# Packed attention and a soft mixture on one core: loads admitted earlier, a new order of the work, and a tail whose first four tiles need no reduction

## The chip, the cores and the metric

One core of one Trainium2 chip. The number is the device time of one execution in microseconds (us), lower is better. Before the change three runs gave 197.42, 199.47 and 200.94 us; the median is 199.47 us.

## The reference

Eight batches, eight heads, 576 tokens, head size 64, all float32. Per head 32 learned rows `p` attend to keys and values, and the 576 queries then attend to those 32 packed rows. The result, laid out as 4608 tokens by 512, goes through a soft mixture of 8 experts with 4 slots each.

```python
p_packed = sm_attn(p, k, v)                    # 32 rows per head
x = sm_attn(q, p_packed, p_packed)             # 4608 x 512 after the transpose of heads
logits = x @ phi                               # 4608 x 32 slots
slot_input = softmax(logits, over tokens).T @ x
slot_out[e] = relu(slot_input[e] @ w1[e]) @ w2[e]      # 512 -> 1024 -> 512, 4 rows per expert
out = softmax(logits, over slots) @ slot_out
```

The weights are 16 MB in `w1` and 16 MB in `w2`; with q, k and v and the output the core moves 72.31 MB.

## The kernel before, in words

The program has two parts. The **attention part** works in eight steps: step i takes two batches and four heads (`k{i}`, `q{i}`, `v{i}`, each in two transfers of 576 KB). Its pieces are functions `f_...`, and the table `ORDER` names them one by one; each piece puts its instructions at the end of its engines' queues, so the table is the order of every engine. A token `s1.3.0@4:a` is piece `s1`, step 3, part 0, PSUM bank 4, copy on ScalarE (`v`: VectorE, `p`: GpSimd). The pieces of a step:

- `kt` turns keys on VectorE; `s1` scores of `p` against keys; `mx1`, `e1` maximum and exponential; `ap`/`apc` turn the weights by TensorE and copy them out; `m` product with values; `ppa`, `pp`, `pt`, `ptc` scale, turn and store the packed rows; `mp`/`mm` their product with `phi`.
- `qp`/`qc` turn queries by TensorE and copy them out; `s2` scores of queries against the packed rows; `mx2`, `sb`, `e2`, `z2`, `rc`, `n2` their softmax (`z2`, `n2` on GpSimd or VectorE); `a2p`/`a2c` turn the result; `lg` adds a step's share of the logits.
- After every second step (a pair) come `f1`, `f2`, `f3`, `f5`, `f6`, `fd`, `fl`, `gz`, `gr`, `rt`, `gt`, `rb`, `gs`, `sa`: the running softmax over tokens and the pair's share of `slot_input`. After the last pair this chain ends in `xz` (line 1076), the input of the first expert layer.
- `w.4.0@7` multiplies ones by ones into a free bank and nothing reads it.

The **expert part** is plain code: `layer1a` and `layer1b` (W1), `layer2` (W2 of experts 0 to 5, 512 columns wide), then `last2` for the last two experts by column halves x = 0 and 1. W2's partial sums stand on four groups of 32 partitions. `total(x)` (VectorE) adds the halves' sums into `so`, `spread(x)` (TensorE, a product with the table `rep`) adds the four groups, and `shared(x)` (ScalarE) copies the result to `sh`. An output tile of 128 tokens is one product of its 32 combine weights `cT` with `sh` (`part`), a copy (`keepp`) and a share of a transfer (`send`). Of the 36 tiles the first 16 are made in column halves, the other 20 whole. `f_cp`/`f_cc` turn the combine weights into `cT`; the third group (`f_cp(2, ...)`) stands after `spread(1)`.

**Loads** are issued by SyncE in one list. The list may run ahead only as far as `ALLOW` says: the products and turns are counted (4 and 2 units), the count passes a mark at 194 and then every 256 units (`FIRST`, `BLOCK`), and entry n of `ALLOW` is the number of transfers that may be issued before mark n + 1 has passed. A transfer also waits for its place: a ring of 120 KB per partition, or, for the weights, places 0 to 5 and x in the work area (`PLACE`), given free by `late.*` and `lx` in `ORDER`; and it waits for the eighth transfer before it. W2 of experts 6 and 7 is loaded by column halves, in rows of 1 KB.

Of the kernel before, what the change touches and what calls it, by code (L numbers as in the profile page):

```python
# [31 lines left out]
ptc.1.1:v ptc.1.0:a z2.0.0:p mp.1.0 mx1.2.0 w.1.0@5 mm.1.0:a s2.1.0@5 kt.3.0 e1.2.0 s2.1.1 kt.3.1
e1.2.1 rc.0.0 ra.2.0 qp.2.1@0 mx2.1.2 qp.2.3@1 n2.0.0:p qc.2.1:a qp.2.2@2 qc.2.3:a ap.2.1@0 qc.2.2:a
kt.3.2 qp.2.0@4 apc.2.1:a qp.2.4@3 sb.1.2 qp.2.5@2 qc.2.0:a a2p.0.0@0 qc.2.4:a qc.2.5:a a2p.0.2@1
a2p.0.1@3 a2c.0.0:a rz.2.0 kt.3.3 ap.2.2@2 e2.1.0 ap.2.0@0 apc.2.2:v s1.3.0@4 a2c.0.1:a z2.1.0:p
s1.3.1 apc.2.0:a a2c.0.2:a m.2.0@2 mx1.3.0 m.2.1 m.2.2 e1.3.0 rc.1.0 e1.3.1 lg.0.0@1 n2.1.0:v
ppa.2.1 ap.3.1@0 ra.3.0 ap.3.0@7 ppa.2.0 apc.3.1:a ap.3.2@6 pp.2.1 apc.3.0:a a2p.1.2@5 kt.4.1
# [1216 lines left out]
```

## Time and profile before

| | |
|---|---|
| time of the profiled execution | 198.95 us |
| its span, first to last instruction | 196.8 us |
| median of three runs | 199.47 us |
| TensorE busy | 167.2 us (85%) |
| VectorE busy | 124.1 us (63%) |
| ScalarE busy | 89.7 us (46%) |
| GpSimd busy | 35.7 us (18%) |
| moved by DMA | 72.31 MB, mean 367 GB/s |

The busy shares are means over stages that have different limits: the attention part ends and the first expert layer starts at about 136 us, the weights are loaded until about 170 us, and from 184 us on only output is moved. So the rows are read by stage, and for each stage the question is which wait ends last.

### The profile page before, as it was taken

The page shows a single profiled execution, that of the slowest core. Times are in us where ns is not written, and L with a number is a line of the kernel's source. Part 1 is how long each engine was busy: PE and PEld are TensorE (multiplying, and loading weights), DVE is VectorE, ACT ScalarE, POOL GpSimd, SP SyncE. Part 2 cuts the span into 40 slices and gives each one's busy share as a digit, 9 for nine tenths or more (in the row PEclk, how much of TensorE's full clock was granted, in tenths as well). Part 3 has the DMA queues.
Part 4 walks back from the last instruction along what each step waited for, and adds up shares of the span by engine and source line. Part 5 has one row for each costly group of instructions (what it writes and reads, how often), then busy time and mean ns, then how long its engine had stood idle before and what let it go on. Part 6 is the DMA issues. An engine that isn't in the chain of part 4 may idle for free.

```text
span 196.8 us, 6563 instructions
## 1 busy us (share of the span) xinstructions
PE 167.2 (85%) x2841; PEld 108.9 (55%) x2841; DVE 124.1 (63%) x261; ACT 89.7 (46%) x229; POOL 35.7 (18%) x61
## 2 busy tenths in 40 slices
PE   7978986999999999999999989687999997979100
...
GB/s 182 377 388 284 388 395 371 214 358 383 390 367 387 394 392 375 354 351 411 410 407 406 342 407 414 417 421 397 382 425 420 399 350 348 205 341 341 441 420 244
DMA packets 29228, 72.31 MB, mean 367 GB/s; under 512 B 2192, under 2 KB 10896, under 8 KB 27408
## 3 DMA queue, kind: packets, MB, share of 16 engines
q1 hardware_dynamic: 29200, 71.90, 97.3%
...
## 4 chain that ended last, share of the span: by engine, by line
PE 34%; DVE 25%; DMA 17%; ACT 9%; issue 3%; SPq 3%; POOL 1%; DVEq 0%; ACTq 0%; POOLq 0%
PE ps L150 31%; DMA ring<-in_k_dram 10%; DMA ring<-in_moe_w_dram 4%; DVE work L448 4%; ACT work L397 4%; PE ps L153 4%; DMA ring<-in_q_dram 3%; DVE work L401 3%; DVE mx L656 3%; SPq L159 3%; DVE ring L401 2%; ACT work L480 2%; DVE nm L477 1%; DVE work L666 1%; DVE zs L716 1%
## 5 line engine op out<-in xcount | busy, mean ns | idle before, releaser
L397 ACT COPY work<-ps 128x512 f32<-128x512 f32 (+3 forms) x68 | 30.0, 487 | 21.7 <-PE ps L153 18.3
L150 PE MATMUL ps<-work 128*64 128x64 f32 (+1 forms) x1088 | 34.0, 313 | 1.7 <-ACT work L397 0.7
L150 PEld LDWEIGHTS ps<-work 128*64 128x64 f32 (+1 forms) x1088 | 24.1, 122 | 10.0 <-issue 2.5
L448 DVE STREAM_TRANSPOSE work<-ring 128x576 f32<-128x576 f32 x32 | 23.3, 755 | 5.9 <-DMA ring<-in_k_dram 5.7
L153 PE MATMUL ps<-ident,ring 128*128 128x128 f32 x144 | 20.6, 280 | 0.1
L150 PE MATMUL ps<-ring,work 64*64 64x128 f32 x576 | 18.3, 273 | 2.2 <-issue 2.0
L150 PEld LDWEIGHTS ps<-ring,work 64*64 64x64 f32 x576 | 15.7, 133 | 4.8 <-issue 3.8
L397 ACT COPY a2Tb<-ps 128x384 f32<-128x384 f32 x21 | 9.8, 497 | 16.5 <-PE ps L153 16.3
L153 PEld LDWEIGHTS ps<-ident,ring 128*128 128x128 f32 x144 | 15.9, 141 | 2.5 <-DVE work L401 0.7
L480 ACT ACTIVATE work<-ps,nm 128x576 f32<-128x576 f32 x16 | 11.8, 739 | 11.9 <-DVE nm L477 11.8
L153 PE MATMUL ps<-ident,work 128*128 128x128 f32 x108 | 15.3, 279 | 1.9 <-ACT work L480 1.5
L656 DVE TENSOR_REDUCE mx<-ps 128x36 f32<-128x1152 f32 (+1 forms) x10 | 11.0, 1100 | 7.5 <-PE ps L150 7.5
L150 PE MATMUL ps<-a,a2Tb 32*128 32x256 f32 (+2 forms) x112 | 13.6, 505 | 2.0 <-DVE a2Tb L401 1.3
L401 DVE COPY ring<-ps 128x256 f32<-128x256 f32 (+1 forms) x25 | 11.3, 514 | 5.7 <-PE ps L150 5.6
L153 PEld LDWEIGHTS ps<-ident,work 128*128 128x128 f32 x108 | 11.8, 141 | 4.9 <-ACT work L480 3.4
L150 PE MATMUL ps<-ring,hT 128*32 128x512 f32 (+1 forms) x136 | 13.2, 496 | 0.3
L397 ACT COPY ring<-ps 128x256 f32<-128x256 f32 (+1 forms) x27 | 10.6, 483 | 5.9 <-PE ps L150 5.9
L150 PE MATMUL ps<-ones 128*128 128x512 f32 (+2 forms) x24 | 12.1, 615 | 1.0 <-DVE ones L118 1.0
L401 DVE COPY work<-ps 128x384 f32<-128x384 f32 (+3 forms) x24 | 11.5, 484 | 2.2 <-PE ps L153 1.8
L150 PE MATMUL ps<-ring,a2Tb 128*32 128x512 f32 x96 | 12.4, 594 | 0.4 <-DVE a2Tb L1076 0.4
L477 DVE TENSOR_REDUCE nm<-ps 128x2 f32<-128x1152 f32 x8 | 10.8, 1349 | 2.6 <-PE ps L150 2.6
L703 POOL TENSOR_TENSOR zt<-work 128x576 f32<-128x576 f32 x3 | 4.3, 1417 | 38.4 <-ACT work L695 38.4
...
## 6 DMA issues: line engine op xcount, KB each, us to landing
ring<-in_moe_w_dram SPq DMA_DIRECT2D x22, 1024.0 KB, 9.3
...
work<-in_moe_w_dram SPq DMA_DIRECT2D x6, 1024.0 KB, 12.2
...
```

Of the source, the lines that this page charges most:

```text
L150: return step(nc.tensor.matmul(*a, **k), 4)
L153: return step(nc.tensor.transpose(*a, **k), 2)
L159: x = nc.sync.dma_start(out=dst, in_=src).ins
L397: nc.scalar.copy(dst, src)
L401: nc.vector.tensor_copy(dst, src)
L448: nc.vector.transpose(kT[:, b2, :, c].rearrange("p m (t r) -> p m t r", t=T), view(f"k{i}.{b2}").rearrange("p (m t c d) -> p m t c d", m=2 ...
L477: nc.vector.tensor_reduce(nms[i % 2], s1v(i), axis=AX.XY, op=ALU.max, negate=True)
L480: nc.scalar.activation(a1[:, :, x].rearrange("p t (h r) -> p h t r", h=2), s1v(i)[:, x].rearrange("p h (t r) -> p h t r", t=T), AF.Exp, bi ...
L656: nc.vector.tensor_reduce(mxs[i % 2][:, a0:a1].rearrange("p a t -> p (a t)"), s2v(i, j).rearrange("p a t s -> p (a t) s"), axis=AX.X, op=A ...
L666: nc.vector.tensor_tensor(a2s[i // NG % 2][:, :, i % NG, a0:a1].rearrange("p t a s -> p a t s"), s2v(i, j), mxs[i % 2][:, a0:a1].unsqueeze ...
L703: nc.gpsimd.tensor_tensor(y, a[:, :, :, 0:w], a[:, :, :, w:NS], op=ALU.add)
L716: nc.vector.reciprocal(z, z)
```

## The change

Four edits. `ALLOW` is raised by 1 or 2 in twelve of its sixteen entries. `ORDER` is written anew (as many pieces; 13 products of ones where 12 stood), and `PLACE` gives places 0 and 1 to other weight chunks. W2 of expert 6 is loaded in one whole first half (rows of 8 KB) and two column halves of the rest. In the tail, `repf` times `cT` gives `wide`, the combine weights of tiles 0 to 3 repeated over 128 partitions; `direct` multiplies them with `so`, so that these tiles need neither `spread` nor `shared`. Twelve tiles are halved instead of 16, in other sends, and all three `f_cp` stand between the `layer2` calls.

```diff
-ALLOW = (24, 24, 24, 27, 31, 34, 39, 43, 47, 51, 55, 57, 60, 62, 64, 66)
+ALLOW = (24, 24, 24, 28, 33, 36, 41, 44, 49, 52, 57, 58, 61, 62, 65, 67)
-PLACE = "rrrrrrrrr01rrr2rr345x"
+PLACE = "rrrrrr01rrrrrr2rr345x"
 ORDER = """
-p.0.0 w.4.0@7 w.1.0@7 px.0.0@0 pc.0.0:a kt.0.0 kt.0.1 kt.0.2 kt.0.3 w.4.0@7 w.4.0@7 w.1.0@7 s1.0.0@0
+p.0.0 w.4.0@7 w.1.0@7 px.0.0@0 pc.0.0:v kt.0.1 kt.0.0 kt.0.3 kt.0.2 w.4.0@7 w.4.0@7 w.1.0@7 qp.0.0@0
...
     cuts = {
-        (E - 2, 0): (0, 4, 8),
+        (E - 2, 0): (4, 8),
         (E - 1, 0): (0, 4, 6, 8),
-        (E - 2, 1): (0, 8),
+        (E - 2, 1): (4, 8),
...
+    f_cp(0, 0, 6, None)
+    f_cc(0, 0, None, "v")
     layer2(3)
+    f_cp(1, 0, 7, None)
+    f_cc(1, 0, None, "a")
     layer2(4)
+    f_cp(2, 0, 4, None)
+    f_cc(2, 0, None, "v")
+    wide = a2f[:, 3 * DM : 4 * DM]
+    for a in range(4):
+        rs = slice(32 * a, 32 * a + 32)
+        product(ps[:, a, 0:P], repf[rs], cT[rs, 0], start=True, stop=True)
+    copy("a", wide.rearrange("p (a x) -> p a x", a=4), ps[:, 0:4, 0:P])
     layer2(5)
+    layer2(E - 2)
...
+    def direct(t, x, b):
+        product(
+            ps[:, b, 0:HB], wide[:, P * t : P * (t + 1)], so[:, halves[x]], start=True, stop=True
+        )
...
+    ends_a = (1, 2, 4, 6, 9, 12)
+    ends_b = (1, 2, 4, 6, 9, 12)
...
+    def lead(x):
+        total(x)
+        direct(0, x, (pa, pb)[x][0])
+        direct(1, x, (pa, pb)[x][1])
+        spread(x)
+        direct(2, x, (pa, pb)[x][2])
+        direct(3, x, (pa, pb)[x][3])
+        keep_tile(0, x, "a")
+        keep_tile(1, x, "v")
+        shared(x)
+        keep_tile(2, x, "v")
+        keep_tile(3, x, "a")
...
     last2(E - 2, 0)
     last2(E - 1, 0)
-    total(0)
-    spread(0)
-    shared(0)
     obs[1] = rows(1)
-    ends_a = (1, 2, 4, 9, 12, 16)
-    ends_b = (2, 4, 9, 16)
+    lead(0)
     tiles(4, 8, 0)
     last2(E - 2, 1)
     tiles(8, 12, 0)
     last2(E - 1, 1)
-    total(1)
-    tiles(12, 16, 0)
-    spread(1)
-    f_cp(2, 0, 4, None)
-    shared(1)
-    tiles(0, 4, 1)
-    f_cc(2, 0, None, "v")
+    lead(1)
```

TensorE at the start of the program, after the first products of ones (`ps<-ones`). `ident,ring` are turns of queries, `work 32x288` are the scores `s1`. Before:

```order
L150 MATMUL ps<-ones 128x512 x2
L150 MATMUL ps<-ones 128x128
L150 MATMUL ps<-work 32x288 x32
L153 MATMUL ps<-ident,ring 128x128 x18
L150 MATMUL ps<-ones 128x512
L153 MATMUL ps<-ident,work 128x128 x9
```

and now:

```order
L150 MATMUL ps<-ones 128x512 x2
L150 MATMUL ps<-ones 128x128
L153 MATMUL ps<-ident,ring 128x128 x9
L150 MATMUL ps<-work 32x288 x16
L153 MATMUL ps<-ident,ring 128x128 x5
L150 MATMUL ps<-work 32x288 x16
L153 MATMUL ps<-ident,ring 128x128 x4
L150 MATMUL ps<-ones 128x512 x2
L153 MATMUL ps<-ident,work 128x128 x9
```

Nine query turns of step 0 moved ahead of its first scores, and two products of ones follow the last query turns where one stood.

VectorE around the softmax of the last step's queries (`mx_172`, `zs_174`), ahead of the last `lg`. `nml`, `nm_176` and `low_137` are `f1` and `f3` of the third pair; `d`, `L_sb` are its `fd`, `fl`. Before:

```order
L764 TENSOR_REDUCE nml<-ps 128x1
L768 SCALAR_TENSOR_TENSOR nm_176<-nml,low_138,own 128x4
L656 TENSOR_REDUCE mx_172<-ps 128x18
L788 TENSOR_REDUCE low_137<-ps 128x1
L666 TENSOR_TENSOR a_1_109<-ps,mx_172 128x2x9x32
L656 TENSOR_REDUCE mx_172<-ps 128x18
L807 STREAM_TRANSPOSE d<-rt 128x288
L666 TENSOR_TENSOR a_1_109<-ps,mx_172 128x2x9x32
L812 STREAM_TRANSPOSE L_sb<-ps 128x288
L700 TENSOR_REDUCE zs_174<-a_1_109 128x9x2 x2
```

and now:

```order
L654 TENSOR_REDUCE mx_172<-ps 128x18
L664 TENSOR_TENSOR a_1_109<-ps,mx_172 128x2x9x32
L654 TENSOR_REDUCE mx_172<-ps 128x18
L664 TENSOR_TENSOR a_1_109<-ps,mx_172 128x2x9x32
L698 TENSOR_REDUCE zs_174<-a_1_109 128x9x2
L713 TENSOR_SCALAR zs_174<-zs_174 128x9x2
L714 RECIPROCAL zs_174<-zs_174 128x9x2
L698 TENSOR_REDUCE zs_174<-a_1_109 128x9x2
L713 TENSOR_SCALAR zs_174<-zs_174 128x9x2
L714 RECIPROCAL zs_174<-zs_174 128x9x2
L718 TENSOR_TENSOR a_1_109<-a_1_109,zs_174 128x9x64
L762 TENSOR_REDUCE nml<-ps 128x1
```

The third pair's chain, which stood between the pieces of this softmax, now follows it.

TensorE behind the last `lg` (`a2Tb,mm_157`), up to the last pair's `gr` (`a_1_109,d`). `work,d` is the third pair's `gr`, `rep,rt` its `gt`, `rb,pp` its `gs`. Before:

```order
L150 MATMUL ps<-a2Tb,mm_157 32x288 x4
L150 MATMUL ps<-ones 128x384
L150 MATMUL ps<-nm_176,rep 128x4
L150 MATMUL ps<-ones 128x512
L150 MATMUL ps<-rw,ones 128x64
L150 MATMUL ps<-a_1_109,d 32x256 x16
```

and now:

```order
L150 MATMUL ps<-a2Tb,mm_157 32x288 x4
L150 MATMUL ps<-rw,ones 128x64
L150 MATMUL ps<-work,d 32x256 x18
L150 MATMUL ps<-nm_176,rep 128x4
L150 MATMUL ps<-rep,rt 64x32 x8
L150 MATMUL ps<-ones 128x256
L150 MATMUL ps<-rb,pp_152 64x64 x2
L150 MATMUL ps<-rb,pp_153 64x64 x2
L150 MATMUL ps<-rw,ones 128x64
L150 MATMUL ps<-a_1_109,d 32x256 x16
```

The third pair's `gr`, `gt` and `gs` stand here now, and two products of ones are gone.

## Rows read from the trace of the kernel before

**Rows 1.** The page, parts 3 and 5: a DMA queue; a group of VectorE copies.
```profile
q1 hardware_dynamic: 29200, 71.90, 97.3%
...
L401 DVE COPY work<-ps 128x384 f32<-128x384 f32 (+3 forms) x24 | 11.5, 484 | 2.2 <-PE ps L153 1.8
```

**Rows 2.** Windows: length, busy us of each engine, TensorE clock, DMA share, GB/s.
```profile
core 0: us, PE busy (x) PEld busy (x) DVE busy (x) ACT busy (x) POOL busy (x), PEclk, DMA share, GB/s
36.00:112.00 76.00, 73.94 (x1607) 58.60 (x1608) 61.04 (x115) 47.08 (x123) 20.41 (x19) 1.00 1.01 376
112.00:136.00 24.00, 19.18 (x297) 12.77 (x299) 17.92 (x48) 11.69 (x33) 7.17 (x9) 1.00 1.02 413
34.00:37.00 3.00, 2.71 (x86) 1.38 (x64) 1.85 (x3) 1.52 (x3) 1.90 (x2) 1.00 0.56 154
80.00:86.00 6.00, 5.85 (x113) 4.17 (x111) 5.14 (x13) 3.83 (x11) 0.00 (x0) 1.00 0.96 321
139.00:155.00 16.00, 16.00 (x164) 5.45 (x160) 8.63 (x23) 2.50 (x5) 0.00 (x0) 1.00 1.01 421
156.00:167.00 11.00, 9.68 (x92) 3.32 (x88) 1.31 (x3) 1.22 (x3) 0.00 (x0) 1.00 1.08 349
168.00:172.00 4.00, 4.00 (x53) 1.84 (x53) 2.26 (x6) 1.46 (x5) 0.00 (x0) 1.00 0.53 178
```

**Rows 3.** The chain that ended last: start us, us, engine, tile, line.
```profile
19.13 8.66 DMA ring<-in_k_dram
...
27.88 0.78 DVE work L448
...
47.87 1.36 DVE work L720
...
116.84 0.32 DVE nml L764
117.19 0.93 DVE nm L768
...
120.58 0.39 DVE d L807
...
121.60 0.39 DVE L_sb L812
...
123.99 0.41 DVE a2Tb L401
...
135.91 16.61 PE ps L150 x160
...
165.09 0.44 DVE a L1133
165.57 0.71 PE ps L150 x2
166.36 0.38 ACT a L397
```

**Rows 4.** Timeline of TensorE: start us, us, line, operation, tiles, count (two instructions per product).
```profile
121.66 1.49 PE L150 MATMUL ps<-work,d 64*32 64x256 f32 x36 [0.26 <-DVE a L666]
...
127.59 0.69 PE L150 MATMUL ps<-a2Tb,mm 128*32 128x288 f32 x8 [0.30 <-ACT a2Tb L397]
...
159.17 1.90 PE L150 MATMUL ps<-ring,hT 128*32 128x512 f32 x16
...
161.81 3.24 PE L150 MATMUL ps<-ring,hT 128*32 128x256 f32 x32
...
168.67 1.07 PE L150 MATMUL ps<-ring,hT 128*32 128x256 f32 x16
...
172.49 0.53 PE L153 MATMUL ps<-ident,L_sb 128*128 128x128 f32 x3
```

**Rows 5.** Waits of SyncE's queue: us in total, times, longest.
```profile
SPq L159 <- PE ps L150: 80.8, 22, 9.4
```

**Rows 6.** DMA issues between 136.9 and 137.2 us: KB, us to landing.
```profile
ring<-in_moe_w_dram SPq DMA_DIRECT2D x1, 1024.0 KB, 5.1
```

More of the change, by code (lines that the diff above doesn't have):

```diff
@@ L32 @@
[L32 to L37, printed above, removed]
@@ new lines @@
+qp.5.4@2 ppa.6.1 ap.7.0@7 qc.5.4:a pp.6.1 ra.7.0 s2.5.0@4 apc.7.0:v ppa.6.0 pp.6.0 rz.7.0 a2p.4.2@7
+pt.6.0 a2c.4.2:a a2p.4.1@2 ptc.6.0:v ptc.6.1:a s2.5.1 a2c.4.1:a mp.6.0 mx2.5.2 qp.6.1@7 mm.6.0:a
+qp.6.3@3 qc.6.1:a qp.6.5@0 qc.6.3:a sb.5.2 qp.6.4@7 qp.6.2@1 qc.6.5:a qp.6.0@2 qc.6.2:a ap.7.1@0
+qc.6.4:v e2.5.0 qc.6.0:v a2p.4.0@6 ap.7.2@7 apc.7.1:v s2.6.1@4 a2c.4.0:a apc.7.2:v z2.5.0:p s2.6.0@6
+mx2.6.1 sb.6.1 qp.7.4@0 qp.7.3@1 qc.7.4:v e2.6.7 mx2.6.0 qp.7.5@5 qp.7.1@0 rc.5.0 lg.2.0@4 qc.7.1:a
@@ new lines @@
+sb.6.0 z2.6.7:p m.7.0@2 qc.7.5:v e2.6.6 m.7.1 late.2.0 qc.7.3:v m.7.2 z2.6.6:p rc.6.7 qp.7.0@1
+ppa.7.1 ppa.7.0 pp.7.1 qp.7.2@0 pp.7.0 qc.7.0:v pt.7.0 qc.7.2:a n2.6.7:p ptc.7.1:v ptc.7.0:a rc.6.6
+s2.7.1@0 n2.6.6:p s2.7.0@5 late.3.0 mx2.7.1 n2.5.0:p sb.7.1 a2p.6.1@7 mx2.7.0 e2.7.7 a2p.6.2@1
+a2p.6.0@0 a2c.6.2:a sb.7.0 mp.7.0 a2c.6.0:a a2p.5.2@1 z2.7.7:v mm.7.0:a e2.7.6 a2p.5.0@0 a2p.5.1@3
+a2c.5.2:a rc.7.7 a2c.5.0:a z2.7.6:v n2.7.7:p a2c.5.1:a a2c.6.1:a rc.7.6 lg.2.1 n2.7.6:v lg.3.0@7
+f1.2.0 a2p.7.1@3 xz.0.0 a2p.7.0@0 a2c.7.1:a f2.2.0 a2c.7.0:a a2p.7.2@6 f3.2.0 f5.2.0 a2c.7.2:v
@@ L1063, in layer2 @@
     def layer2(e):
-        for j in range(NJ):
+        for j in range(NJ if e < E - 2 else NJ // 2):
             a = j % 4
@@ L1124, in last2 @@
                 w2h(e, j, x),
-                start=(e == E - 2 and j < 4),
+                start=(e == E - 2),
                 stop=(e == E - 1 and j >= 4),
@@ L1167, in send, with keep_tile, tiles @@
         nc.sync.dma_start(out=ov[:, t0:t1, xs], in_=ob[:, t0:t1, xs])
+    def direct(t, x, b):
+        product(
+            ps[:, b, 0:HB], wide[:, P * t : P * (t + 1)], so[:, halves[x]], start=True, stop=True
+        )
+    pa = (4, 6, 7, 5, 0, 4, 6, 7, 5, 0, 2, 4)
+    pb = (6, 7, 5, 0, 2, 4, 1, 6, 7, 5, 0, 2)
+    NA = len(pa)
+    ends_a = (1, 2, 4, 6, 9, 12)
+    ends_b = (1, 2, 4, 6, 9, 12)
+    def keep_tile(t, x, eng):
+        keepp(t, x, (pa, pb)[x][t], eng)
+        ends = (ends_a, ends_b)[x]
+        if t + 1 in ends:
+            send(max(n for n in (0, *ends) if n <= t), t + 1, x)
+    def tiles(t0, t1, x):
+        for t in range(t0, t1):
+            part(t, x, (pa, pb)[x][t])
+        for t in range(t0, t1):
+            keep_tile(t, x, "av"[t % 2])
+    def lead(x):
[10 more added lines that the diff above has]
+        keep_tile(3, x, "a")
     nc.vector.tensor_copy(sot[:, halves[0]], ps[:, SO, halves[0]])
@@ L1196, in pack_attention_soft_moe @@
     last2(E - 1, 1)
-    total(1)
-    tiles(12, 16, 0)
-    spread(1)
-    f_cp(2, 0, 4, None)
-    shared(1)
-    tiles(0, 4, 1)
-    f_cc(2, 0, None, "v")
-    for t in range(4, NA, 4):
-        tiles(t, t + 4, 1)
-    obank = (0, 2, 4, 6, 7, 5, 1, 3)
+    lead(1)
+    tiles(4, 8, 1)
+    tiles(8, 12, 1)
+    obank = (3, 4, 1, 6, 7, 5, 0, 2)
     work = {"a": 0.0, "v": 0.0}
```

100 lines of the change are left out of this document (39 added, 61 removed).

## The prediction, made before the changed kernel ran

> **What bounds the kernel now.** I read the DMA queues first, then the windows by stage, then the chain of waits, then the timeline of TensorE around the two ends of the expert part. The queue of the loads is occupied 97.3% of the span [rows 1], so the first guess is that bytes set the time. The windows say how far that is true: the DMA moves 421 GB/s with rows of 8 KB, 349 with rows of 1 KB, and falls to 154, 321 and 178 in short stretches [rows 2]. Against 376, the mean of 36 to 112 us, these hold idle time of 3 x (1 - 154/376) = 1.8 and 6 x (1 - 321/376) = 0.9 us, and, against 349, 4 x (1 - 178/349) = 2.0 us. SyncE spends most of its waiting on TensorE's products, 80.8 us in 22 waits [rows 5]: `ALLOW` and the places hold loads back, no lack of data.
>
> The chain decides what such a wait costs. Until 27.8 us it consists of transfers that wait for no product; from 27.88 to 152.5 us no transfer stands in it, only TensorE, VectorE, ScalarE and GpSimd [rows 3]. So computation sets the start of layer 1, which I call S (135.91), and the weights that need a place freed by layer 1 start only after it. Within that stretch TensorE is busy 73.94 of the 76 us from 36 to 112 and 19.18 of the 24 us from 112 to 136 [rows 2]. Behind S both bind: TensorE's last products ahead of `total(0)` take 3.24 us for 32 instructions where 16 of the same shape take 1.07 [rows 4], so 1.1 us of them is waiting for the last weights, and the end is the DMA sending output.
>
> The sums stand against the profiled execution, 198.95 us (its span is 196.8); the median of three runs is 0.52 higher, and the forecast is the median less the gain.
>
> **Loads further ahead.** Before S they fill up to 1.8 + 0.9 = 2.7 us of idle DMA. I count 0 for it: no step between 27.9 us and S waits for a transfer, so this work hides it entirely; were computation to become faster by more than that, the cover would be gone and loads would be late next. Behind S it shortens the queue that the last weights stand in: a transfer of 1 MB issued just after S lands 5.1 us later [rows 6], while its bytes at 421 GB/s take 2.5. The gain there lies between 0 and 2.6 us; I take 1.4, about the middle, since a transfer into an empty queue needs some time too before its bytes flow.
>
> **The order up to S.** At the start nine query turns precede the first scores, so these begin later, by the wait for q and the turns. Nothing for it, as the chain waits for the keys of step 2 until 27.8 us in any case; without that cover it would cost the turns and the wait, some 2 us. From 36 to 112 us the same products and turns run in another order on an engine that idles 2.06 us there; I take 0, between a gain of 2.06 and a loss by VectorE. That loss is bounded by the copies: VectorE gets 13 more of them (13 x 0.484 = 6.3 us by its mean copy [rows 1]) and gives up two `n2` (2 x 1.36 [rows 3]), a `z2` of that size and one half as large (2.0), net 1.6 us.
>
> From 112 us to S something moves that stands in the chain. Between the scores of the last queries and the last `lg` (127.59 [rows 4]) VectorE now works off, in the chain, `f1` of the third pair (0.32 + 0.93), its `fd` and `fl` (0.39 + 0.39) and a copy for `lg` (0.41), together 2.44 us [rows 3]. The copy goes to ScalarE; the rest moves behind the softmax. `f1` comes back ahead of the last `lg`, as 0.6 us: -1.8. The last scores also start earlier, since nine turns (`a2p` of step 5) and one `lg` move behind them; one `lg` is 0.69 us [rows 4], and the way through `m`, `pp`, `pt`, `ptc` doesn't shrink, so I take -0.9. Behind the last `lg`, S follows after 135.91 - 127.59 = 8.3 us. The third pair's `gr` now stands on TensorE in there, ahead of the last pair's `f2`: 1.49 us [rows 4], of which the 0.6 of `f1` would be waited for anyway, so +0.9; with two products of ones gone I take +0.8. `gt` and `gs` stand where TensorE waits for the last pair's `f3` and `f5`, and I count them at 0; without that cover they cost their own length. Sum: S - 1.9, between -4.0 (with the 2.06) and +1.6.
>
> **From S to `total(0)`.** It starts at S + 29.18 now (165.09); without its 1.1 us of waiting TensorE would be there at S + 28.1. Added on TensorE: the third group of `cT` turns (0.53), the four products for `wide` (at most the 0.53 of four products of 256 columns) and four products of 512 columns instead of 256 (0.95 - 0.53) [rows 4]: S + 29.6. By the loads it would be 29.18 - 1.4 + 1.0 (1 MB of whole rows, 2.5 us at 421, lands ahead where 0.5 MB of half rows, 1.5 us at 349, did) = 28.8, at worst 30.2. TensorE is the later one: +0.4.
>
> **From `total(0)` to the end.** Two things. One MB of output leaves in whole rows: 3.0 us at 349 against 2.5 at 421, -0.5. The Trainium skill says in "DMA: Bandwidth & Descriptors", Specifications, that transfers reach line rate from 512 B on, so rows of 1 KB should lose nothing and this term would be 0. The trace shows 349 against 421 here and disagrees; by the rule the forecast would be 0.5 us higher. Second, idle DMA at 168 to 172 us, 2.0 us: outputs are not ready. The first tiles now skip `spread` and `shared` (166.74 - 165.57 = 1.2 us in the chain [rows 3]), tiles 4 and 5 leave without tile 8, and the third `cp` with its copy no longer stands in front of the second half's tiles. Some idle time stays between the small sends: I take -1.0, between 0 and -2.0. Together -1.5.
>
> **Sum:** -1.9 + 0.4 - 1.5 = -3.0: 195.9 in the frame of the profiled execution, 199.5 - 3.0 = **196.5 us** against the median.
>
> **Rivals.**
> 1. Nothing gained before S. For it: TensorE at 97% over 76 us can't be beaten by order, and the third pair's chain comes back between the last `lg` and S, in full if it doesn't overlap. Against it: 2.44 us of VectorE in the chain have left. Time: 0.4 - 1.5 = -1.1: 198.4. That the loads don't run ahead in effect, because the place or the eighth transfer before stops them, ends here too.
> 2. The whole order is better. The 2.06 us of idle TensorE between 36 and 112 us go as well, S - 4.0, which the 2.7 us of filled DMA and the queue behind S allow in part. For it: VectorE is busy only 61 of those 76 us, so its waits are latency, and latency is what an order changes. Against it: little idle time is left to take. Time: -4.0 + 0.4 - 1.5 = -5.1: 194.4.
> 3. Slower: VectorE becomes the bound in the attention part. In-order copies ahead of `mx2`, `kt` and `nm` delay `s1` and `s2`, the added 6.3 us fall on the path and the removed 4.7 us lie off it. It decides as soon as TensorE's idle time in the 76 us grows past the 1.1 us that the tail gives back. Price up to 6.3 - 1.1 = +5.2, 204.7; halfway, +3.2 - 1.1, 201.6. For it: in the whole stretch from 36 us to S VectorE has 79 of 100 us already. Against it: ScalarE's share goes down by as many copies.
>
> **Chances and range.** Forecast 0.45, rival 1 0.22, rival 2 0.21, rival 3 0.12. A measurement of this kernel tells about 2% from no change, which is 195.5 and 203.5 us. Faster: nearly all of rival 2 and 0.3 of the forecast, whose own spread (the idle time after `total(0)`, the queue at S) is about 1.2 us either way: 0.34. Slower: the upper half of rival 3, 0.06. Within: 0.60. The range for 8 in 10 takes in rivals 1 and 2 with their spread and leaves out most of rival 3 and the far end of rival 2: 193.2 to 200.0.
>
> **What would show it.** S near 134 us, with the last `lg` about 9 us ahead of it and no `f1`, `fd`, `fl` in the chain between the last scores and the last `lg`; DMA windows without the drops to 154 and 321 GB/s; TensorE without a gap before `total(0)`, which comes 29.6 us after S; 31.7 - 1.5 = 30.2 us from `total(0)` to the end of the span. It is wrong if S is at 136 or later, if the chain between 28 us and S holds transfers again, or if the DMA still idles 2 us after the weights.

## The result, and the profile after the change

The changed kernel took **199.89 us** (median of 22 runs), the kernel before 198.61 us beside it (22 runs): a ratio of 1.0063, 95% interval [1.0038, 1.0088]. I had forecast 196.5 us, so the change went 1.3 us up where I had it 3 us down. The 3.0 were taken off the median of three runs, 199.47; off the 198.61 of 22 runs the same forecast would be 195.6. Some executions of every kernel take a few per cent longer than its others: the ratios leave them out, and the only profile of e12_max_first, below, is of such a one, so its S is not given. The profiled execution of the changed kernel has a span of 197.7 us (before 196.8).

The windows of the changed kernel, the stages of [rows 2] and four more; columns as there:

```profile
36.00:112.00 76.00, 70.87 (x1566) 56.38 (x1569) 60.66 (x121) 44.57 (x116) 25.38 (x23) 1.00 1.01 377
112.00:136.00 24.00, 18.62 (x331) 12.98 (x323) 17.87 (x50) 10.31 (x29) 9.23 (x11) 1.00 0.99 390
34.00:37.00 3.00, 3.00 (x77) 1.74 (x55) 2.36 (x4) 0.97 (x3) 2.06 (x3) 1.00 0.94 286
80.00:86.00 6.00, 5.51 (x137) 3.80 (x113) 5.42 (x12) 2.66 (x10) 0.00 (x0) 1.00 1.01 376
95.00:98.00 3.00, 3.00 (x114) 2.42 (x114) 2.23 (x5) 0.48 (x1) 1.29 (x2) 1.00 0.47 98
128.00:131.00 3.00, 2.38 (x42) 1.37 (x24) 1.54 (x8) 1.60 (x6) 0.00 (x0) 1.00 0.80 262
139.00:155.00 16.00, 16.00 (x164) 5.77 (x160) 8.68 (x24) 2.50 (x5) 0.00 (x0) 1.00 1.01 419
156.00:167.00 11.00, 10.39 (x98) 3.76 (x99) 1.96 (x4) 1.44 (x3) 0.00 (x0) 1.00 1.06 365
168.00:172.00 4.00, 4.00 (x46) 2.04 (x44) 2.29 (x6) 2.04 (x6) 0.00 (x0) 1.00 0.61 206
172.00:178.00 6.00, 5.29 (x44) 4.17 (x42) 3.15 (x8) 2.78 (x8) 0.00 (x0) 1.00 0.78 256
```

The two drops of the DMA that the loads ahead were to fill are filled (34 to 37 us: 154 to 286 GB/s; 80 to 86 us: 321 to 376). But new ones stand further on, 98 GB/s at 95 to 98 us and 262 at 128 to 131 us, and the one after the weights is there still (206, before 178), followed by another at 172 to 178 us. TensorE has lost 3.1 us of busy time between 36 and 112 us (73.94 to 70.87) and GpSimd has gained 5.0 (20.41 to 25.38).

TensorE in the timeline of the changed kernel, at the end of the attention part and at `total(0)`; a bracket gives the idle time ahead of a row and what ended it:

```profile
115.94 2.32 PE L150 MATMUL ps<-work 128*64 128x64 f32 x72 [1.02 <-ACT work L395]
...
122.27 1.18 PE L150 MATMUL ps<-a2Tb,mm 128*32 128x288 f32 x16 [0.94 <-ACT a2Tb L395]
124.07 0.85 PE L153 MATMUL ps<-ident,a 128*128 128x128 f32 x6 [0.63 <-DVE a L718]
...
126.23 0.69 PE L150 MATMUL ps<-a2Tb,mm 128*32 128x288 f32 x8 [0.81 <-DVE a2Tb L399]
...
127.34 1.49 PE L150 MATMUL ps<-work,d 64*32 64x256 f32 x36
...
129.76 0.66 PE L150 MATMUL ps<-rep,rt 128*64 128x32 f32 x16 [0.62 <-ACT rt L395]
...
135.98 1.51 PE L150 MATMUL ps<-ring,a2Tb 128*32 128x512 f32 x12 [0.45 <-DVE a2Tb L1074]
...
161.46 4.72 PE L150 MATMUL ps<-ring,hT 128*32 128x512 f32 x48
166.76 1.13 PE L150 MATMUL ps<-a 128*128 128x256 f32 x4 [0.58 <-DVE a L1138]
```

The last `lg` moved from 127.59 [rows 4] to 126.23, and S stands at 135.98 where it was 135.91 [rows 3]: what was won ahead of the last `lg` came back behind it. The last products ahead of `total(0)` take 4.72 us for 48 instructions, 24 of 512 columns and 24 of 256; by the 1.90 and 1.07 us that 16 of either take [rows 4] that would be 2.85 + 1.61 = 4.5 us, so TensorE waits little here. But its last four, at 165.56, follow the landing of the last weights of x = 0, 256 KB issued at 156.01 (first row below; KB and us to landing), at 165.51. `total(0)` starts at 166.29 (chain rows below) where it was 165.09 [rows 3].

```profile
ring<-in_moe_w_dram SPq DMA_DIRECT2D x1, 256.0 KB, 9.5
```

```profile
165.56 0.65 PE ps L150 x4
...
166.29 0.43 DVE a L1138
166.76 5.46 PE ps L150 x50
```

### The profile page after: what moved, and what is told of

Read it like the earlier page. It is cut to its first block, busy times and chain, and to the rows that moved or that the text cites. A ratio compares the mean times of both kernels' runs of the same rounds, so it can differ in the third digit from the quotient of the medians.

```text
span 197.7 us, 6582 instructions
## 1 busy us (share of the span) xinstructions
PE 166.0 (84%) x2835; PEld 110.8 (56%) x2835; DVE 127.1 (64%) x270; ACT 85.1 (43%) x215; POOL 44.3 (22%) x69
## 4 chain that ended last, share of the span: by engine, by line
PE 49%; DVE 24%; ACT 7%; issue 5%; POOL 5%; DMA 3%; SPq 1%; DVEq 0%; ACTq 0%; POOLq 0%
PE ps L150 39%; PE ps L153 10%; DVE nm L475 5%; DMA ring<-in_q_dram 3%; DVE work L446 3%; ACT work L478 3%; DVE work L399 2%; POOL a L718 2%; DVE ring L399 2%; DVE mx L654 2%; DVE a L664 1%; DVE work L664 1%; DVE zs L714 1%; ACT work L395 1%; POOL work L718 1%
## 5 line engine op out<-in xcount | busy, mean ns | idle before, releaser
L395 ACT COPY work<-ps 128x512 f32<-128x512 f32 (+3 forms) x55 | 24.7, 488 | 23.2 <-PE ps L153 20.7
L150 PE MATMUL ps<-work 128*64 128x64 f32 (+1 forms) x1088 | 32.0, 313 | 1.2 <-ACT work L395 1.0
L150 PEld LDWEIGHTS ps<-work 128*64 128x64 f32 (+1 forms) x1088 | 23.0, 121 | 6.6 <-issue 2.5
L399 DVE COPY work<-ps 128x512 f32<-128x512 f32 (+3 forms) x37 | 17.8, 498 | 6.7 <-PE ps L153 5.2
L153 PE MATMUL ps<-ident,ring 128*128 128x128 f32 x144 | 20.1, 279 | 2.3 <-DMA ring<-in_q_dram 2.0
L153 PE MATMUL ps<-ident,work 128*128 128x128 f32 x108 | 16.1, 278 | 3.4 <-ACT work L478 2.5
L153 PEld LDWEIGHTS ps<-ident,ring 128*128 128x128 f32 x144 | 15.7, 141 | 5.7 <-DVE work L446 2.1
L701 POOL TENSOR_TENSOR zt<-work 128x576 f32<-128x576 f32 x4 | 5.7, 1419 | 55.2 <-ACT work L693 48.2
L399 DVE COPY ring<-ps 128x256 f32<-128x256 f32 (+1 forms) x23 | 11.4, 544 | 5.5 <-PE ps L150 5.3
L395 ACT COPY ring<-ps 128x512 f32<-128x512 f32 (+1 forms) x25 | 10.4, 524 | 6.6 <-PE ps L150 6.6
L150 PE MATMUL ps<-ones 128*128 128x512 f32 (+3 forms) x26 | 11.6, 556 | 1.0 <-DVE ones L118 1.0
L150 PE MATMUL ps<-a,a2Tb 32*128 32x512 f32 (+2 forms) x88 | 11.4, 549 | 0.0
```

The costliest lines, as they stand in the source:

```text
L150: return step(nc.tensor.matmul(*a, **k), 4)
L153: return step(nc.tensor.transpose(*a, **k), 2)
L395: nc.scalar.copy(dst, src)
L399: nc.vector.tensor_copy(dst, src)
L701: nc.gpsimd.tensor_tensor(y, a[:, :, :, 0:w], a[:, :, :, w:NS], op=ALU.add)
```

## The experiments

Eighteen runs, two of which repeat a kernel (e9 and e17), stand each beside the kernel before on the same chip, in five groups on five chips: e1, e2, e3, e5; e4, e6, e7, e8; e9 to e11; e12 to e15; e16 to e18. The change itself ran with the third group alone (e9), besides its 22 runs above, so a distance between it and a kernel of another group is less certain than one inside a group. On the chip of e4, e7 and e8 the kernel before has its lowest median (197.84 us; 198.34 to 198.90 on the other four). Three numbers were read from each one's trace: S, the time from S to `total(0)`, and from `total(0)` to the landing of the last output. "Idle DMA" is worked out from the packets in the trace: time, in 16 engines, without a packet in flight.

| kernel | order to 108 us / end / tail | ratio to before, 95% interval | S | S to `total(0)` | to the end |
|---|---|---|---|---|---|
| before | old / old / old | 1 | 135.91 | 29.18 | 30.73 |
| after | new / new / new | 1.0063 [1.0038, 1.0088] | 135.98 | 30.31 | 30.31 |
| e9_again | the same kernel | 1.0071 [1.0036, 1.0107] | 136.48 | 29.89 | 30.32 |
| e1_tail | old / old / new | 0.9986 [0.9951, 1.0021] | 135.18 | 30.20 | 29.48 |
| e2_order | new / new / old | 1.0021 [0.9988, 1.0055] | 135.77 | 28.65 | 31.07 |
| e3_old_end | new / old / new | 1.0120 [1.0077, 1.0163] | 137.31 | 30.54 | 30.27 |
| e5_new_end | old / new / old | 0.9958 [0.9923, 0.9993] | 135.05 | 29.53 | 31.13 |
| e17_end_again | the same kernel as e5 | 1.0025 [0.9985, 1.0065] | 134.26 | 29.70 | 31.08 |
| e10_end_tail | old / new / new | 0.9997 [0.9960, 1.0034] | 135.02 | 30.16 | 29.56 |
| e18_end_half | as e10, half rows | 0.9998 [0.9964, 1.0032] | 134.50 | 29.29 | 29.91 |
| e14_end_whole | as e5, whole rows | 1.0037 [1.0003, 1.0071] | 135.25 | 31.22 | 31.04 |
| e13_old_to_95 | old to 95 us / new / new | 1.0023 [0.9994, 1.0051] | 135.74 | 30.44 | 30.33 |
| e6_allow | before, new ALLOW | 1.0028 [0.9994, 1.0062] | 134.63 | 28.81 | 30.90 |
| e7_old_places | after, old PLACE | 1.0103 [1.0048, 1.0158] | 136.02 | 30.52 | 30.30 |
| e15_old_loads | after, old ALLOW and PLACE | 1.0161 [1.0118, 1.0203] | 137.40 | 30.42 | 30.32 |
| e4_half_rows | after, half rows | 1.0126 [1.0075, 1.0176] | 136.29 | 30.62 | 30.74 |
| e8_sixteen | after, sixteen halved tiles | 1.0127 [1.0081, 1.0173] | 136.46 | 30.25 | 31.00 |
| e11_vector | after, four pieces on VectorE | 1.0164 [1.0123, 1.0204] | 137.97 | 29.90 | 30.29 |
| e12_max_first | after, one maximum moved | 1.0010 [0.9978, 1.0043] | - | - | - |
| e16_first_old_tail | as e12, old tail | 1.0036 [1.0000, 1.0073] | 136.65 | 28.85 | 31.06 |

One reading comes before all others. The piece at which the orders are exchanged, the maximum of step 6's first query scores, starts at 106 to 110 us in the traces (108.06 in the changed kernel); the 103 us of the expectations below is the maximum of step 5. In eight profiles with the old order up to there (before, e1, e5, e6, e10, e14, e17, e18) S lies between 134.26 and 135.91, mean 135.0; in seven with the new one (after, e2, e4, e7, e8, e9, e15) between 135.77 and 137.40, mean 136.3 (136.2 without e15). The seven all have the new end too; of the eight, the five with the new end have 134.8. The profile of the kernel before happens to be the latest of its group: its chain begins with keys that land at 27.79 us [rows 3], and the same keys land at 27.28 in this chain of e10_end_tail:

```profile
18.72 8.56 DMA ring<-in_k_dram
```

So two profiles alone, 135.91 against 135.98, hide that the new order makes S some 1.4 us **later** with the same end (134.8 against 136.2). A profile is of one execution, and those with an S here lie up to 1.3 us from the median of their kernel (e6 1.3 below, e14 1.3 above), so a single S carries as much doubt; the two groups don't depend on it, and the ratios say the same inside one group: e10_end_tail 0.9997, e9_again 1.0071.

**The parts one by one.** e1_tail is the kernel before with the new tail, e2_order the kernel before with the new tables:

```diff
 e1_tail, against after:
-PLACE = "rrrrrr01rrrrrr2rr345x"
+PLACE = "rrrrrrrrr01rrr2rr345x"
 and ALLOW and ORDER of before
 e2_order, against before:
-PLACE = "rrrrrrrrr01rrr2rr345x"
+PLACE = "rrrrrr01rrrrrr2rr345x"
 and ALLOW and ORDER of after
```

> The kernel before with the new tail alone (expert 6 loaded as one whole first half and two column halves, `direct`, twelve halved tiles, the new sends); ORDER, ALLOW and PLACE are the old ones, so the start of layer 1 (S) should stay within 0.3 us of 135.9. Theory T (the tail is what made the change slower): the whole-row half of expert 6 puts 0.5 MB more ahead of the last weights of x = 0, `total(0)` comes 1.0 us later than before's S + 29.2, the later part gives back 0.3, and the time is 0.7 us over before's 198.6: 199.3. Theory O (the order is what made it slower, the tail gains): `total(0)` no later than S + 29.6, and 1.0 to 1.5 us under before: 197.1 to 197.6.

> The kernel before with the new ORDER, ALLOW and PLACE; the tail is the old one. Theory T: S at 136.0 as in both kernels, then `total(0)` at S + 29.2 as before, the time 198.6, within 0.3 us of before. Theory O: S at 136.0, but the lead of the loads is lost at S, the weights behind it come late, `total(0)` at S + 30 or later, and the time is 199.5 to 200.0, about 1 us over before.

Measured: 0.9986 and 1.0021, neither distinguishable from before. Theory T is wrong in its price, theory O in its stage: in e1_tail `total(0)` is 1.0 us later behind S, as T says, but the end is 1.25 us nearer to it (29.48 against 30.73); in e2_order nothing is lost behind S.

e3_old_end and e5_new_end exchange the order from step 6's first `mx2` on (two score banks renamed):

```diff
 e3_old_end: ORDER of after up to
   ... s2.6.1@0 s2.6.0@5 mx2.6.1
+  then the pieces left, in the order of before: lg.2.0@7 m.7.0@2 rc.5.0 qp.7.3@4 mx2.6.0 ...
 e5_new_end: ORDER of before up to
   ... s2.6.1@4 s2.6.0@6 mx2.6.1
+  then the pieces left, in the order of after: sb.6.1 qp.7.4@0 qp.7.3@1 qc.7.4:v e2.6.7 ...
```

> The changed kernel; from the maximum of step 6's first query scores on (103 us) its remaining pieces run in the order of the kernel before (two score banks renamed as there). Theory E (the new end of the attention part gains nothing, since what it takes out ahead of the last `lg` comes back behind it): the last `lg` again about 11.4 us after the last scores and S 8.3 us after it; S within 0.4 us of the 136.0 of the changed kernel, the time within 0.4 us of its 199.9. Theory P (my prediction: the new end is worth 1.9 us, and the gain was lost earlier): S at 137.5 to 138, the time 201 to 202.

> The kernel before; from the maximum of step 6's first query scores on its remaining pieces run in the new order (two score banks renamed as there). Theory E: S within 0.4 us of 135.9, the time within 0.4 us of before's 198.6. Theory P: S at 134.0 to 134.5, the time 197.0 to 197.5.

> The kernel before with the new end of the attention part alone, once more, on another chip. If the gain is real: 0.2 to 0.6% below before, S at 134.8 to 135.3. If it was chance: within 0.2% of before.

The new end is worth 1.1 us where the rest is new (one profile, S 137.31, against a mean of 136.2 without e15) and 0.4 us where the rest is old (mean of the five with the new end 134.8, of before, e1 and e6 135.2). It lies between E (0) and P (1.9). The 0.4% that e5_new_end showed did not come again in e17_end_again.

**The loads.**

```diff
 e6_allow, against before:
-ALLOW = (24, 24, 24, 27, 31, 34, 39, 43, 47, 51, 55, 57, 60, 62, 64, 66)
+ALLOW = (24, 24, 24, 28, 33, 36, 41, 44, 49, 52, 57, 58, 61, 62, 65, 67)
 e7_old_places, against after:
-PLACE = "rrrrrr01rrrrrr2rr345x"
+PLACE = "rrrrrrrrr01rrr2rr345x"
 e15_old_loads, against after: both lines as before
```

> The kernel before with the raised ALLOW alone. Theory Q (my prediction: a lead of the loads shortens the queue behind S by 1.4 us): the weights behind S land 1.4 us earlier and the time is 197.2 to 197.5, where before has 198.7. Theory C (the lead can't be carried over S: the transfers ahead of S go into places 0 to 5 and x, which the attention part frees, and the first one behind S waits for layer 1 itself): the DMA idles less up to 92 us (4 us or less, before 5.3) and as much more from 92 to 140 us (1.5 or more, before 0.5), the weights behind S land within 0.3 us of before's, time within 0.4 us of before's.

> The changed kernel with the old PLACE: places 0 and 1 are given to the tenth and eleventh weight transfer again instead of the seventh and eighth. Theory C (a cap): the 1.6 us of idle DMA at 92 to 112 us shrink to 0.8 or less, but places 4 and 5 come free no earlier, the DMA idles correspondingly more at 112 to 140 us (2.0 us, changed kernel 1.25), the weights behind S land within 0.3 us of the changed kernel's, time within 0.4 us of its 199.9. Rival Q (the places 0 and 1 taken too early lose the lead): those weights land 0.8 us or more earlier relative to S, time 199.1 or less.

> The changed kernel with the old ALLOW and the old PLACE; order and tail are the new ones. Theory V (the order is what costs, and the loads' lead is worth nothing): S at 135.8 to 136.5, the DMA idles about 2 us more up to 92 us and 1 us less from 92 to 140 us, time within 0.3% of the changed kernel. Rival A (the raised ALLOW costs, by loads that run beside the other work): S at 135.3 or earlier, time 0.3% or more below the changed kernel. Rival Q (the lead is worth 1.4 us): time 0.7% above the changed kernel.

Windows of e6_allow, and under them the same of the kernel before:

```profile
28.00:66.00 38.00, 35.88 (x818) 27.66 (x817) 30.78 (x55) 22.67 (x59) 10.24 (x10) 1.00 1.04 383
128.00:140.00 12.00, 10.08 (x132) 4.52 (x136) 7.22 (x23) 2.95 (x9) 1.83 (x1) 1.00 0.89 332
```

```profile
28.00:66.00 38.00, 34.34 (x768) 26.05 (x768) 30.70 (x54) 22.07 (x58) 9.28 (x9) 1.00 0.98 357
128.00:140.00 12.00, 10.08 (x130) 4.57 (x126) 6.71 (x22) 2.95 (x9) 1.83 (x1) 1.00 1.00 396
```

What the raised ALLOW wins from 28 to 66 us (357 to 383 GB/s) it mostly gives back from 128 to 140 (396 to 332). Idle DMA by stage, in us:

| | 0-92 us | 92-128 | 128-140 | 166-178 |
|---|---|---|---|---|
| before | 5.3 | 0.4 | 0.2 | 2.0 |
| e6_allow | 3.2 | 0.5 | 1.4 | 1.6 |
| after | 2.9 | 1.6 | 1.3 | 3.4 |
| e7_old_places | 3.3 | 4.1 | 0.1 | 3.2 |
| e15_old_loads | 5.2 | 1.2 | 0.0 | 3.1 |

Theory C holds in its mechanism and not in all its numbers. In e6 the DMA idles as it said, and the weights behind S land 0.4 us earlier relative to S; its time is not told apart from before's. In e7 the DMA sums went against it: 4.1 us of idle DMA at 92 to 112 us instead of 0.8 or less. Up to 140 us the kernels before and after idle the same 5.8 us. The transfers ahead of S go into places that the attention part frees, and the first transfer behind S waits for layer 1: it was issued at 136.99 before, with 2 MB under way (1 MB of it landed 0.09 us later), and at 137.05 after, with 1 MB under way, and landed at 142.07 and 142.85.

The 10 us behind S show where the lead goes, first in the kernel before, then in the changed one:

```profile
135.91:145.91 10.00, 9.99 (x96) 3.47 (x100) 6.33 (x17) 1.92 (x4) 1.46 (x1) 1.00 1.00 397
```

```profile
135.98:145.98 10.00, 10.00 (x96) 3.47 (x100) 6.37 (x18) 1.92 (x4) 1.45 (x1) 1.00 0.96 376
```

In this stretch the DMA moved 364 to 385 GB/s in the nine profiles with the lead (after, e2, e3, e4, e6, e8, e9, e11, e16) and 397 to 414 in the ten without it (the old ALLOW, or e7, which lost it): 33 GB/s or 0.33 MB less in the mean, of the 0.47 MB more that had landed at S. With the new tail nothing is left of the lead behind S: S to `total(0)` is 30.31 and 29.89 with it, 30.42 without (e15), 30.52 with it lost at 92 to 112 us (e7). With the old tail some is: 28.65 to 28.85 in the three kernels with the raised ALLOW (e2, e6, e16), 29.18 to 29.70 in the three without (before, e5, e17), 0.7 us in the mean. Why the new tail loses it is not shown. e15_old_loads is 0.9% slower than the change (on another chip); that is near rival Q's price, but all of it lies ahead of S (137.40), where none of the three expectations had it; in its stretch from the second pair's `lg` to the `mx2` of step 6 it took 27.97 us where the six others with this order took 27.1 to 27.2. Why is open. That the new order has less cover ahead of S shows in four chains, which contain keys that land behind 36 us (36.5 in e7, 36.8 in e8, 37.1 in e16, 39.07 in e9_again, the row below); before, no transfer behind 27.9 us stood in it:

```profile
27.73 11.34 DMA ring<-in_k_dram
```

**The middle of the attention part.** TensorE's largest new gap, 1.4 us at 76 us, ends with an `n2` that the change gave to GpSimd.

> The changed kernel itself, unchanged, so that its distance to the kernel before is known on the chip on which the next two run, and so that a second profile shows how far S and the stages vary without any edit: S within 0.5 us of 136.0, time 0.4 to 1.0% over before.

> The kernel before with the two parts of the change that alone came out below it: the new end of the attention part (from the maximum of step 6's first query scores on) and the new tail; the order up to there, ALLOW and PLACE are the old ones. Theory M (the new order of the middle, up to 103 us, is what cost the gains of the rest): S at 134.5 to 135.3, time 0.4 to 0.8% below before. Rival I (new end and new tail hinder each other, as the weights in places 4 and 5 come 5 us later with the one and the whole rows want them early with the other): at or over before's time, up to +0.5%.

> The changed kernel with the four pieces that it moved from VectorE to GpSimd (`n2` of steps 1 and 3, `z2` of step 4, one half `z2` of step 6) back on VectorE. Theory G (TensorE waits for GpSimd there: 2.13 us for an `n2` and 2.8 for a `z2`, where VectorE takes 1.3 to 1.4): TensorE's 1.38 us gap at 76 us and half of the other idle time from 36 to 92 us go, S 0.8 to 1.4 us earlier than the changed kernel's, time within 0.3% of before. Rival V (VectorE is the bound): its added 5 us appear as later copies, S at 136.0 or later, time as the changed kernel's.

```diff
 e11_vector, against after (ORDER):
-n2.1.0:p  n2.3.0:p  z2.4.0:p  z2.6.7:p
+n2.1.0:v  n2.3.0:v  z2.4.0:v  z2.6.7:v
 e10_end_tail: ORDER of e5_new_end, ALLOW and PLACE of before, tail of after
```

e10_end_tail is at 0.9997 with S at 135.02: S is as theory M has it, the time only at before's, where rival I had it. Beside e9_again (1.0071) it is 0.7% faster, so the order up to 108 us, with its ALLOW and PLACE, costs that; and it is the order more than the loads, as the new order with the old ALLOW and PLACE is no faster (e15, 1.0161) and the new ALLOW with the old order is at 1.0028 (e6). e11_vector is at 1.0164 with S at 137.97: theory G is wrong, and the time is rival V's or worse. Its TensorE at the gap, and its chain further on:

```profile
76.64 1.20 PE L153 MATMUL ps<-ident,a 128*128 128x128 f32 x9 [0.93 <-DVE S_run L929]
```

```profile
93.94 1.35 DVE zs L698
95.30 0.34 DVE rt L399
...
95.66 0.38 ACT rt L395
...
113.43 0.66 DVE zs L698
```

The two `n2` neither cost nor gain: the gap shrinks from 1.39 to 0.93 us, yet the second pair's `lg` starts at 81.39, in e9_again at 81.38. The loss is the two `z2` (`zs`, 1.35 and 0.66 us): on VectorE they stand in the chain, the first ahead of `rt`, for which TensorE then waits 1.23 us instead of 0.23. VectorE in e9_again, ahead of the gap, and TensorE beside it:

```profile
70.89 1.43 DVE L446 STREAM_TRANSPOSE work<-ring 128x576 f32<-128x576 f32 x2
72.24 0.39 DVE L902 TENSOR_TENSOR rb<-ps,hm 128x256 f32<-128x256 f32 x1
72.55 0.28 DVE L712 TENSOR_REDUCE zs<-zt 128x36 f32<-128x144 f32 x1
72.87 0.18 DVE L713 TENSOR_SCALAR zs<-zs 128x36 f32<-128x36 f32 x1
73.08 0.38 DVE L714 RECIPROCAL zs<-zs 128x36 f32<-128x36 f32 x1
73.38 1.29 DVE L475 TENSOR_REDUCE nm<-ps 128x2 f32<-128x1152 f32 x1
74.59 0.28 DVE L929 COPY S_run<-ps 128x128 f32<-128x128 f32 x1
74.78 2.09 DVE L446 STREAM_TRANSPOSE work<-ring 128x576 f32<-128x576 f32 x3
```

```profile
73.06 2.20 PE L150 MATMUL ps<-ring,work 64*64 64x128 f32 x72
76.65 1.17 PE L153 MATMUL ps<-ident,a 128*128 128x128 f32 x9 [1.39 <-POOL a L718]
```

No row of VectorE has idle time ahead of it: the reciprocal that `n2` waits for stands behind two key turns (1.43 us) and `rb`. GpSimd is only the last link of that chain, and that this place costs S anything is not shown (e11 took its `n2` off GpSimd and did not reach the second pair's `lg` earlier). TensorE is busy 23.60 us of 66 to 92 us here and 25.31 in e10_end_tail.

The second place is the maximum of step 6's scores, behind three key turns:

```diff
 e12_max_first, against after (ORDER); e16_first_old_tail: the same with the old tail
-s1.6.1 kt.7.0 kt.7.2 mp.4.0 lg.1.0@5 mm.4.0:a kt.7.1 lg.1.1 mx1.6.0
+s1.6.1 kt.7.0 mx1.6.0 kt.7.2 mp.4.0 lg.1.0@5 mm.4.0:a kt.7.1 lg.1.1
 e13_old_to_95: ORDER of before up to mx1.7.0, the rest and the tail of after, ALLOW, PLACE of before
```

> The changed kernel with one piece moved: the maximum of step 6's scores (`mx1.6.0`) stands on VectorE behind one turn of step 7's keys (`kt`) instead of three. Theory V (VectorE is the bound there; in the changed kernel this maximum ends 2.6 us after the logits of the second pair start, 1.1 us later than with the old order, and TensorE then waits 0.6 us for the exponential): the maximum starts 1.0 to 1.4 us earlier, S 0.5 to 1.0 us earlier than in the changed kernel (135.2 to 135.7), time 0.3 to 0.5% below it, so 0.2 to 0.4% over before. Rival K (the turns of the keys only come later, and step 7's scores wait for them; or the stretch is not where it is lost): S and time as the changed kernel's, 0.6 to 0.8% over before.

> The old order (with the old ALLOW and PLACE) up to the maximum of step 7's key scores at 95 us, the new order from there on, and the new tail; e10_end_tail keeps the old order until 103 us. Theory V (the loss arises ahead of 95 us): S at 134.8 to 135.3 and time within 0.3% of before, as e10_end_tail. Rival L (it arises between 95 and 103 us): S at 135.7 or later, time 0.5 to 0.8% over before, as the change.

> New order, new ALLOW and new PLACE with the maximum of step 6's scores moved ahead of two key turns as in e12_max_first, and the old tail (e2_order had this without the move: 0.2% over before, S at 135.77). Theory V (VectorE's queue around 80 us was the larger part of the new order's loss): S at 134.8 to 135.3, time 0.2 to 0.6% below before. Rival K (the gain of e12_max_first has another source, or was chance): S at 135.7 or later, time as e2_order or over it.

TensorE behind the step's scores, first in e9_again, then in e16_first_old_tail:

```profile
84.69 0.39 PE L150 MATMUL ps<-nm,rep 128*128 128x4 f32 x2
85.65 0.87 PE L153 MATMUL ps<-ident,work 128*128 128x128 f32 x6 [0.58 <-ACT work L478]
```

```profile
85.56 0.39 PE L149 MATMUL ps<-nm,rep 128*128 128x4 f32 x2
85.80 0.85 PE L152 MATMUL ps<-ident,work 128*128 128x128 f32 x6
```

The gap is gone (in e12's profile too). From the second pair's `lg` to step 6's first `mx2`, stretches in which nearly the same products run, it is 27.18 us in after, e9 and e2, 26.47 in e16, and 26.2 to 26.7 in the five kernels with the old order and the new end. So this one piece holds 0.7 us of that stretch, and e12_max_first (1.0010) is 0.6% below the change, on another chip. In e12's own profile the stretch still takes 27.14 us, with a pause of 0.49 us in the products behind the `lg`. And e16_first_old_tail came out as rival K has it (1.0036, S 136.65; e2 1.0021): its second pair's `lg` already starts at 82.25, where the others of the new order have 80.7 to 81.5. It is late from its first `lg` on (45.85 us, the others 44.6 to 45.6), 35 us ahead of the moved piece, so the lateness is not the piece's; but a gain in time was seen with e12 alone. e13_old_to_95 lies between its two expectations (1.0023, S 135.74): its second pair's `lg` is late (81.44, with the old order 80.6 in the mean), but the stretch takes 26.46 us in it, so the loss of 0.7 us arises ahead of 95 us.

**The tail.**

```diff
 e4_half_rows (against after), e18_end_half (against e10_end_tail):
-        (E - 2, 0): (4, 8),
+        (E - 2, 0): (0, 4, 8),
-        (E - 2, 1): (4, 8),
+        (E - 2, 1): (0, 8),
 e14_end_whole, against e5_new_end: the same lines the other way round
 e8_sixteen, against after:
-    ends_a = (1, 2, 4, 6, 9, 12)
+    ends_a = (1, 2, 4, 9, 12, 16)
-    ends_b = (1, 2, 4, 6, 9, 12)
+    ends_b = (2, 4, 9, 16)
     last2(E - 1, 1)
+    total(1)
+    tiles(12, 16, 0)
     lead(1)
```

> The changed kernel with W2 of expert 6 loaded wholly in column halves again (rows of 1 KB, as in the kernel before); `direct`, the twelve halved tiles and their sends stay. Theory T (the whole-row half is what delays `total(0)` and with it the end): the last weights of x = 0 land 28.5 us after S instead of 29.5, `total(0)` at S + 29.3 instead of S + 30.3, time 199.0 or less, 0.8 to 1.0 under the changed kernel's 199.9. Rival B (behind S the end is set by the bytes that the DMA has still to move and by how long it idles, so bringing 0.5 MB behind `total(0)` only changes the order of the bytes): `total(0)` 1.0 us earlier all the same, the last load no earlier, 0.5 us more for the 1 KB rows, time 199.9 to 200.4.

> The changed kernel with sixteen halved tiles again and the sends of the kernel before; the tiles 12 to 15 of x = 0 run while VectorE makes `total(1)`, as before; `direct` and the whole-row half stay. Theory R (what the new tail loses is the DMA's idle time behind 172 us: twelve tiles leave nothing to send while `total(1)` is awaited, and the six sends of x = 1 are small): idle DMA at 172 to 178 us 0.3 or less instead of 1.4, time 198.9 or less, 1.0 under the changed kernel. Rival T (the tail's loss is `total(0)`, 1.1 us late): the idle time shrinks but the end follows `total(0)`, and the time is within 0.4 us of the changed kernel's 199.9.

> The kernel before with the new end of the attention part and, of the new tail, the whole first half of expert 6 alone; tiles and sends are the old ones. Theory W (a transfer's rate behind S is what counts: 0.5 MB more in whole rows saves 0.25 us, while `total(0)` comes 1.0 us later, when the DMA has other weights to move): DMA idle time at 166 to 178 us up by less than 0.5, time 0.2 to 0.6% below before. Rival T (the later `total(0)` leaves the DMA without outputs): idle time there up by 1 us, time as before or 0.3% over it.

> e10_end_tail (old order to 103 us, new end, new tail: 0.0% against before) with expert 6 by column halves again. Theory T (the whole-row half brings x = 0's last weights 1.0 us later and the DMA then idles for lack of outputs): x = 0's last weights land at S + 28.5 instead of S + 29.4, `total(0)` follows, time 0.3 to 0.8% below before. Rival B (the bytes are only moved about, and 1 KB rows cost 0.25 us per 0.5 MB): time 0.0 to 0.3% over before.

e18_end_half shows theory T's mechanism: with half rows `total(0)` comes at S + 29.29 instead of 30.16, and idle DMA at 166 to 178 us is 2.1 us instead of 3.2. Its time is not lower than e10_end_tail's (0.9998 and 0.9997), as rival B says. e14_end_whole shows it from the other side: `total(0)` at S + 31.22, 2.7 us of idle DMA at 166 to 172 us where e5_new_end has 1.8, 1.0037. e4_half_rows did not repeat it (30.62), and its 1.0126 is over both expectations: its weights came later from the first transfers behind S on (the fourth landed 16.3 us behind S, 14.6 in after), where its edit changes nothing, and why is not shown. e8_sixteen refutes theory R: its idle time at 172 to 178 us stays at 1.3 us; its 1.0127 is over rival T's price too, and what makes this second gap is open.

No version ran reliably below the kernel before; e1, e10, e12 and e18 equal it.

## Why the prediction was wrong

The forecast of -3.0 and the +1.3 measured lie 4.3 us apart: 1.4 in the order from 36 to 112 us, taken as 0; 0.8 to 1.5 in the end of the attention part; 0.7 from S to `total(0)`, by the lead of the loads; 0.6 behind it.

**Bounds.** That computation sets S held, nearly (keys stand in four chains). At the start the nine turns cost nothing, as I had it: the maximum of step 2's key scores starts at 34.5 to 35.1 us in the seven new, at 34.4 to 35.8 in the eight old. That behind S TensorE would be the later one at `total(0)` failed: the weights are. TensorE's own figure was right: by the spacing of its last products (0.215 us for four instructions of 256 columns) `total(0)` would start at S + 29.7 in after and e9_again, an estimate from their rows, where I had 29.6.

**Loads ahead: -1.4, measured 0** (with the new tail; -0.7 with the old). The lead at S was 0.47 MB, and most of it was lost behind S, as the DMA ran short of transfers there. I took the middle between 0 and 2.6 without asking where the led transfers go: into places freed at 96, 112, 118, 128 and 133 us. The step that failed is "behind S it shortens the queue that the last weights stand in". My 0 ahead of S held for the old order only (e6 gained nothing); with the new one the old ALLOW costs 0.9%.

**Order from 36 to 112 us: 0, measured +1.4** (134.8 to 136.2 with the same end). Of it 0.5 us arise up to 81 us (the second pair's `lg` starts at 80.6 in the mean of the eight old, at 81.1 in the seven new), 0.7 from there to step 6's `mx2`, the rest behind it. The step that failed is "I take 0, between a gain of 2.06 and a loss by VectorE": I had bounded that loss with counts of VectorE's operations, net 1.6 us, and looked for none of the places at which TensorE waits for VectorE. Sums and busy shares don't show them: VectorE is busy 60.66 of the 76 us after and 61.04 before, while TensorE's idle time there went from 2.06 to 5.13 us. For the 0.7 the runs show which piece stands behind which (the maximum behind three key turns: e16's trace, e12's time, e13); for the 0.5 they don't, as e11 shows that the `n2` at 76 us is not it. Rival 3 named this place and this mechanism, but priced it from the operations' sum (3.2 to 5.2 us) and met it with a tail that was to give 1.1 back.

**112 us to S: -1.9, measured -0.4 to -1.1.** Last scores to last `lg` shrank by 1.1 us (11.4 to 10.3) where I had 1.8: VectorE's 2.44 us left the chain, but TensorE still waits there, 0.94 us for a copy of ScalarE and 0.63 for VectorE. The last scores came 0.3 us earlier instead of 0.9, since they still wait 1.02 us for a copy (first row above). Behind the last `lg` it takes 9.75 us instead of 8.33, +1.4 where I had +0.8: the third pair's `gt`, which I counted at 0, waits 0.62 us for its copies, and what the last pair has to do stands behind it.

**S to `total(0)`: +0.4, measured +1.1.** My own figure by the loads without the lead is 29.18 + 1.0 = 30.2; 30.31 and 29.89 were measured, the last weights landing at S + 29.53 and S + 29.11. The term fell with the loads' 1.4.

**`total(0)` to the end: -1.5, measured -0.9** (mean 30.1 over the nine new tails with whole rows and twelve tiles, 31.0 over the six old ones). Here the two halves went opposite ways. Fewer bytes in rows of 1 KB save more than my 0.5: span less idle DMA is 185.9 us in the mean of the nine and 187.0 in the six, -1.1, since 1 MB of weights counts as well as 1 MB of output; single profiles spread as widely (184.9 to 187.2 and 186.3 to 187.9). The idle DMA, which I took from 2.0 down to 1.0, went up: at 166 to 178 us from 1.8 in the six to 3.2 in the nine. The first output leaves 1.61 us behind `total(0)` instead of 2.82, the 1.2 us that I had priced, but `total(0)` stands only 3.6 us ahead of the end of the loads instead of 5.1, and between 172 and 178 us each transfer issued finds 0.5 to 1.0 MB under way, where before it was 1.0 to 1.75 MB. So the "-1.0" failed: an earlier first tile does not fill a queue that runs dry because the stage ahead of it came late (e18: with `total(0)` 0.9 us nearer to S the idle time at 166 to 172 us is 1.1 us instead of 2.1).

**Sum:** +1.4 (middle) - 0.4 (end of the attention part, with the old order) + 1.1 - 0.9 = +1.2; measured +1.3. The parts run alone don't add up to it: the new tail gives -0.14% (e1), the new tables +0.21% (e2), both together +0.6 to 0.7%. Some 1.1 us are missing; by the profiles 0.7 of it is the lead of the loads, which shows behind S with the old tail alone, and the rest is open. Rival 1 had S right in the two profiles and missed the tail. The sign was rival 3's, and the chance of 0.12 for it was too low.
